# Pooled attention and a gated spatial MLP on one core: the last tokens' scores of two pairs join the second pair's, and the order tables are written anew

## The chip, the cores and the metric

One core of a Trainium2 chip runs the whole program. The metric is the device time of one execution in microseconds, from runs on the chip; the median of three runs of the kernel before is the reference point.

The engines are named as in the profile: PE (matrix multiplications; PEld is its weight loads), DVE (vector), ACT (scalar and activation), POOL (general purpose) and SP, which issues all transfers.

## The reference

```python
# q, k, v: (8 batches, 8 heads, 576 tokens, 64)
k_p = k.reshape(B, H, 72, 8, 64).mean(axis=3)      # keys pooled by 8
v_p = v.reshape(B, H, 72, 8, 64).mean(axis=3)      # values pooled by 8
scores = np.matmul(q, k_p.transpose(0, 1, 3, 2)) / 8
attn = np.exp(scores - scores.max(-1, keepdims=True))
attn = attn / (attn.sum(-1, keepdims=True) + 1e-9)
x = np.matmul(attn, v_p)            # then (8, 576, 512), heads side by side
h = np.maximum(x @ w_in, 0)         # 512 -> 1024
u, v = h[..., :512], h[..., 512:]
v_n = (v - v.mean(-1)) / np.sqrt(v.var(-1) + 1e-6)
v_s = np.einsum('ts,bsd->btd', w_spatial, v_n) + b_spatial[:, None]
out = (u * v_s) @ w_out             # 512 -> 512
```

## The kernel before

**Tiles.** Each of the eight batches goes through attention and then through the MLP. Eight heads make four pairs (g = 0 to 3), two pairs make a j. The 576 tokens are four tiles of 128 and a last piece of 64 (`TL`). There are 72 pooled keys (`SP`). Most products are made of a high and a low part in fp32r, so a value is first rounded (ACT writes the high part, DVE or POOL the low one); scores and transposes are plain fp32.

**Stages.** Each stage is a Python generator, and each `yield` cuts it into steps. `K` and `V` load keys and values and pool them by 8: on PE with `^` behind the name (`pool_pe`: eight matmuls with the identity, L302), on DVE or POOL otherwise (`pool_sum`: three additions, L291 and L296). `KT` transposes the pooled keys into `kT`. `Q0` to `Q3` load a pair's queries and transpose them: `qT` for the four full tiles, `ql` (tile `pt_q`) for the last 64 tokens of the pairs of one j.

`S0` to `S3` (`att_softmax`, L501) make the scores of a pair's four tiles, sixteen matmuls of 64 x 64, into the PSUM tile `s_ps`, and take the softmax. `U0` and `U1` (`att_softmax_l`, L514) do the same for the last 64 tokens of the two pairs of one j: four matmuls into `s_ps` and a softmax of their own. Each `S` and each `U` so has a maximum, exponentials, a sum, a reciprocal (DVE and ACT), one multiplication on POOL (L490), and a copy of the last columns. With a mark behind the name (`S2~`) the exponentials run on ACT straight from `s_ps`, one instruction for each of the eight (or two) rows of a tile; without it DVE first subtracts the maximum and ACT takes one instruction. There is one `s_ps` (two banks), so a group of scores waits until the softmax ahead of it has read the one before.

`T` and `Y` transpose the weights of attention (through DRAM, from batch 2 on), `W` rounds the values, `A00` to `A13` (L647 to L650) multiply them into `xT`. In the MLP, `v0` to `v4` (L699, L715) make the v half and its normalisation (the power on POOL, L686; the low part `vn_l` on POOL, L709), `u` (L742) the u half, `s` (L761 to L763) the spatial product and the gate, `o` (L784) the output. `wv`, `wu`, `wo`, `ws` load the weights; with `^` the low part is made on PE (L223 to L225), without it on POOL.

**Order.** Nothing is scheduled by a tool: `manual_schedule` keeps, on each engine, the order in which the program is written. That order is three tables of stage names: `FIRST` (start, weights and batches 0 and 1), `STEP` (run for each batch 1 to 6) and `LAST` (batch 7). Each name runs the next step of that stage; `+` and `-` shift the batch, and a name whose generator has ended does nothing. So an instruction stands in its engine's queue where the table puts it, and waits there, with all that is behind it, until its operands are ready.

Of the kernel before, what the change touches and what calls it, by code (L numbers as in the profile page):

```python
# [8 lines left out]
F32 = mybir.dt.float32  # L9
# [68 lines left out]
def pooled_attention_gmlp(ctx: ExitStack, tc: tile.TileContext, q, k, v, w_in, w_sp, b_sp, w_out, out):  # L78
    nc = tc.nc
    B, H, S, D = q.shape  # L80
    P = 128
# [216 lines left out]
    def pool_pe(st, dst):  # L298

        m = dst.shape[0]  # L300
        for j in range(POOL):
            nc.tensor.matmul(dst, lhsT=ident[:m, :m], rhs=st[:, :, j * D:(j + 1) * D], start=j == 0, stop=j == POOL - 1)  # L302
# [562 lines left out]
```

## Time and profile before

| what | us |
|---|---|
| median of three runs (556.33 to 556.9) | 556.41 |
| the profiled execution's own time | 556.75 |
| its span in the trace | 554.9 |
| PE busy in the span | 539.7 |
| DVE busy | 374.7 |
| ACT busy | 291.6 |
| POOL busy | 229.4 |

The time of an execution lies 1.85 us above the span of its trace. An engine's busy time is the union of its instructions: matmuls overlap one another, so a stretch in which PE is always busy can still be shortened, by fewer columns or fewer breaks between groups. The distance from one start to the next shows this, not the duration of one instruction.

### The profile page before, as it was taken

The page shows a single profiled execution, that of the slowest core. Times are in us where ns is not written, and L with a number is a line of the kernel's source. Part 1 is how long each engine was busy: PE and PEld are TensorE (multiplying, and loading weights), DVE is VectorE, ACT ScalarE, POOL GpSimd, SP SyncE. Part 2 cuts the span into 40 slices and gives each one's busy share as a digit, 9 for nine tenths or more (in the row PEclk, how much of TensorE's full clock was granted, in tenths as well). Part 3 has the DMA queues.
Part 4 walks back from the last instruction along what each step waited for, and adds up shares of the span by engine and source line. Part 5 has one row for each costly group of instructions (what it writes and reads, how often), then busy time and mean ns, then how long its engine had stood idle before and what let it go on. Part 6 is the DMA issues. An engine that isn't in the chain of part 4 may idle for free.

```text
span 554.9 us, 11870 instructions
## 1 busy us (share of the span) xinstructions
PE 539.7 (97%) x4297; PEld 479.1 (86%) x4297; DVE 374.7 (68%) x930; ACT 291.6 (53%) x916; POOL 229.4 (41%) x316
## 2 busy tenths in 40 slices
PE   4899999999999999999999999999999999999997
PEld 4687788988998889988998889988998889989995
DVE  4589999879766286869687586869687675544010
ACT  3598679743635545373645546364645565425221
POOL 3636754864654234342424224342525126117130
PEclk9999999999999999999999999999999999999999
DMA  8958525537604317342555327342634420201102
GB/s 239 277 180 178 134 90 118 140 102 240 150 11 109 129 45 197 94 126 79 133 140 155 121 57 209 89 127 68 147 87 124 141 57 26 58 0 39 40 1 96
DMA packets 123355, 63.11 MB, mean 114 GB/s; under 512 B 84256, under 2 KB 104736, under 8 KB 123296
## 3 DMA queue, kind: packets, MB, share of 16 engines
q1 hardware_dynamic: 123296, 62.35, 41.8%
q8 instruction: 34, 0.56, 0.4%
q14 instruction: 25, 0.20, 0.1%
HBM read 44.92 MB, written 17.40 MB: 112 GB/s over the span
## 4 chain that ended last, share of the span: by engine, by line
PE 89%; DVE 5%; ACT 2%; DMA 1%; issue 1%; POOL 1%; SPq 1%; DVEq 0%; ACTq 0%
PE mm L761 19%; PE mm L784 18%; PE mm L742 17%; PE mm L699 16%; PE s_ps L501 4%; PE mm L715 2%; PE tp L647 2%; PE mm L762 2%; PE mm L763 2%; PE tp L650 1%; PE tp L649 1%; PE tp L648 1%; DMA st<-in_k 1%; PE mm L302 1%; PE s_ps L514 1%
## 5 line engine op out<-in xcount | busy, mean ns | idle before, releaser
L742 PE MATMUL mm<-xT,win_h 128*128 128x320 f32 (+1 forms) x512 | 104.1, 298 | 0.4 <-DVE wT_l L167 0.4
L775 POOL TENSOR_TENSOR gT<-g,gT 128x256 fp32r<-128x256 f32 x64 | 47.1, 745 | 125.4 <-ACT gT L772 125.3
L742 PEld LDWEIGHTS mm<-xT,win_h 128*128 128x128 f32 x512 | 81.9, 188 | 3.0 <-DVE wT_l L167 0.6
L699 PE MATMUL mm<-win_h,xT 128*128 128x512 f32 x256 | 80.4, 395 | 0.0
L784 PE MATMUL mm<-wout_h,gT 128*128 128x512 f32 x256 | 80.4, 395 | 0.0
L761 PE MATMUL mm<-wT_h,vn_h 128*128 128x256 f32 (+1 forms) x256 | 76.5, 299 | 0.0
L761 PE MATMUL mm<-wT_l,vn_h 128*128 128x256 f32 (+1 forms) x256 | 75.5, 295 | 0.0
L761 PE MATMUL mm<-wT_h,vn_l 128*128 128x256 f32 (+1 forms) x256 | 75.4, 294 | 0.0
L742 PE MATMUL mm<-xT,win_l 128*128 128x256 f32 (+1 forms) x256 | 75.1, 293 | 0.0
L490 POOL TENSOR_TENSOR e<-e,rs 128x576 f32<-128x576 f32 (+1 forms) x48 | 44.3, 924 | 72.2 <-DVE rs L488 36.5
L483 ACT ACTIVATE e<-s_ps,mx 128x72 f32<-128x72 f32 x164 | 50.1, 332 | 20.3 <-DVE mx L469 18.7
L699 PEld LDWEIGHTS mm<-win_h,xT 128*128 128x128 f32 x256 | 47.1, 188 | 10.2 <-ACT win_l L227 0.2
L784 PEld LDWEIGHTS mm<-wout_h,gT 128*128 128x128 f32 x256 | 46.9, 188 | 9.9
L686 POOL TENSOR_TENSOR rstd<-rstd,neg_half 128x1 f32<-128x1 f32 (+1 forms) x40 | 24.8, 622 | 70.1 <-DVE rstd L684 70.1
L766 DVE TENSOR_TENSOR g<-mm,ru 128x256 f32<-128x256 f32 (+1 forms) x64 | 28.0, 447 | 36.1 <-PE mm L763 33.6
L167 DVE TENSOR_TENSOR xT<-tp,xT 128x320 fp32r<-128x320 f32 (+1 forms) x64 | 28.5, 447 | 33.2 <-ACT xT L165 32.8
L709 POOL TENSOR_TENSOR vn_l<-vv,vn_h 128x512 fp32r<-128x512 f32 x32 | 41.6, 1316 | 21.9 <-ACT vn_h L707 21.8
L784 PE MATMUL mm<-wout_l,gT 128*128 128x512 f32 x128 | 50.4, 394 | 0.0
L699 PE MATMUL mm<-win_l,xT 128*128 128x512 f32 x128 | 50.3, 393 | 0.0
L761 PEld LDWEIGHTS mm<-wT_h,vn_h 128*128 128x128 f32 x256 | 48.1, 188 | 1.0 <-DVE wT_l L285 0.3
L761 PEld LDWEIGHTS mm<-wT_h,vn_l 128*128 128x128 f32 x256 | 48.2, 188 | 0.1
L761 PEld LDWEIGHTS mm<-wT_l,vn_h 128*128 128x128 f32 x256 | 48.1, 188 | 0.0
(186 smaller groups left out, 1231.2 us busy)
## 6 DMA issues: line engine op xcount, KB each, us to landing
st<-in_k SPq DMA_DIRECT2D x32, 256.0 KB, 4.1
out<-ob SPq DMA_DIRECT2D x32, 256.0 KB, 2.0
qt<-in_q SPq DMA_DIRECT2D x112, 72.0 KB, 2.5
st<-in_v SPq DMA_DIRECT2D x24, 256.0 KB, 3.3
xd<-X SPq DMA_DIRECT2D x24, 256.0 KB, 2.9
pt_l<-xd SPq DMA_DIRECT2D x24, 256.0 KB, 3.4
stw<-in_moe_w_in SPq DMA_DIRECT2D x8, 512.0 KB, 5.7
st<-in_moe_w_out SPq DMA_DIRECT2D x4, 512.0 KB, 7.3
```

Source lines behind the costliest of these rows:

```text
L167: nc.vector.tensor_tensor(lo, src, f32(hi), op=ALU.subtract)
L483: nc.scalar.activation(em[:, h, :], sv[:, h % 2, h // 2, :], AF.Exp, bias=mx[:, h:h + 1], scale=QK, accum_out=sm[:, h:h + 1])
L490: nc.gpsimd.tensor_tensor(em, em, rs.unsqueeze(2).broadcast_to([m, n, SP]), op=ALU.mult)
L501: nc.tensor.matmul(s_ps[i * TL:(i + 1) * TL, e, c * SP:(c + 1) * SP], lhsT=t["q", g][es, at:at + TL], rhs=kT[es, g, :], start=True, stop=True)
L686: nc.gpsimd.tensor_tensor(rstd[:m], rstd[:m], neg_half[:m], op=ALU.pow)
L699: nc.tensor.matmul(a, lhsT=xT[:, i, o + c * P:o + (c + 1) * P], rhs=w[:, i, DH:], start=(i == 0 and j == 0), stop=(i == NK - 1 and j == 2))
L709: nc.gpsimd.tensor_tensor(t["vn_l"][:, c, :], vv, f32(t["vn_h"][:, c, :]), op=ALU.subtract)
L742: nc.tensor.matmul(a, lhsT=w[:, i, d * P:(d + 1) * P], rhs=xT[:, i, o + ts.start:o + ts.stop], start=(i == 0 and j == 0), stop=(i == NK - ...
L761: nc.tensor.matmul(a, lhsT=x[:, c, ds], rhs=y[:, c, ts], start=(c == 0 and j == 0), stop=False)
L766: nc.vector.tensor_tensor(g, a, t["ru"][:, d, ts], op=ALU.mult)
L775: nc.gpsimd.tensor_tensor(dst[:, d, 1, at:at + m], g[:, o:o + m], f32(dst[:, d, 0, at:at + m]), op=ALU.subtract)
L784: nc.tensor.matmul(a, lhsT=src[:, i, x, at:at + m], rhs=w[:, i, :], start=(i == 0 and j == 0), stop=(i == ND - 1 and j == 2))
```

## The change

The stages `U0` and `U1` are gone. `S1` and `S3`, the scores of the second pair of each j, have a fifth tile: the last 64 tokens of both pairs of that j, from `ql`. It lies in the same `s_ps`, and one softmax takes all ten rows of a tile; the tiles `mx`, `e`, `sm` and `rs` grow from eight to ten. `S0` and `S2` stay as they were.

```diff
     def att_softmax(t, g, alt=""):
...
-        for c in range(NC):
+        j, odd = divmod(g, 2)
+        n = NC + odd
+
+        for c in range(n):
             for i in range(2):
                 for e in range(2):
                     es, at = slice(e * D, (e + 1) * D), c * P + i * TL
-                    nc.tensor.matmul(s_ps[i * TL:(i + 1) * TL, e, c * SP:(c + 1) * SP],
-                                     lhsT=t["q", g][es, at:at + TL], rhs=kT[es, g, :], start=True, stop=True)
-        yield
-        em = yield from softmax(s_ps[:, :, :4 * SP].rearrange("p e (c s) -> p e c s", s=SP), P, 8, alt)
-        nc.gpsimd.tensor_copy(new_pr(t, g // 2)[:, :NC, :, g % 2], em[:, 1::2, SP - KR:])
-        t["p", g] = em
-
-    def att_softmax_l(t, j, alt=""):
-
-        sl = ps.tile([P, 2, 512], F32, name="s_ps", tag="s")
...
+                    lhs, pair = (t["q", g][es, at:at + TL], g) if c < NC else (t["ql", j][es, i, :], 2 * j + i)
+                    nc.tensor.matmul(s_ps[i * TL:(i + 1) * TL, e, c * SP:(c + 1) * SP], lhsT=lhs, rhs=kT[es, pair, :],
+                                     start=True, stop=True)
+        yield
+        em = yield from softmax(s_ps[:, :, :n * SP].rearrange("p e (c s) -> p e c s", s=SP), 2 * n, alt)
+        pr = new_pr(t, j)
+        nc.gpsimd.tensor_copy(pr[:, :NC, :, odd], em[:, 1:2 * NC:2, SP - KR:])
+        t["p", g] = em[:, :2 * NC, :]
+        if odd:
+            nc.gpsimd.tensor_copy(pr[:TL, NC, :, 0], em[:TL, 2 * NC + 1, SP - KR:])
+            yield
+            nc.scalar.copy(pr[:TL, NC, :, 1], em[TL:, 2 * NC + 1, SP - KR:])
+            t["pl", j] = em[:, 2 * NC:, :]
```

A new mark `%` for `K` and `V` would halve the pooling on PE by one addition ahead of it; the new tables give it to no `K` and no `V`, so `pool_half` adds nothing here. The three tables are written anew. The first entries of `FIRST`:

```diff
-    "wv0 wv0 wv0 -K^ wv3~^ -K -K wv3 wv0 -K wv3 wv0 -Q1^ wo1^! -K wv3 -K wv0 -Q0~^ wv3 -K -KT -Q0 wo1 wo1 -KT "
+    "wo1~ -K^ -K wo1 wo1 wo1 -K wv1 -Q0~^ -K wv1 wo1 -K -Q0 wv1 -K wo1 -K wv3^! wv3 -Q1^ wv1 wv1 -KT~ -Q0 -KT "
```

By the new tables five weight chunks instead of six are rounded on PE (three matmuls fewer: `x`, a high part and `z`), and pooling moves between engines: of the halves of `K` and `V` that are summed by `pool_sum`, DVE has 6 instead of 22 and POOL 18 instead of 2. What is pooled on PE stays the same in number.

**PE in the middle of the program, before.** `pt_q` holds the last tokens' queries, `qT` the other tokens'; the wide products with `xT` belong to the stages `u` and `v`.

```order
L742 MATMUL mm<-xT,win_h 128x256 x2
L742 MATMUL mm<-xT,win_l 128x256
L514 MATMUL s_ps<-kT,pt_q 64x72 x4
L742 MATMUL mm<-xT,win_h 128x320 x2
L742 MATMUL mm<-xT,win_l 128x320
```

The same place in the change:

```order
L734 MATMUL mm<-win_h,xT 128x512
L734 MATMUL mm<-win_l,xT 128x512
L530 MATMUL s_ps<-kT,qT 64x72 x16
L530 MATMUL s_ps<-kT,pt_q 64x72 x4
L761 MATMUL mm<-xT,win_h 128x320 x2
L761 MATMUL mm<-xT,win_l 128x320
```

The four matmuls of the last tokens now follow the sixteen of the second pair, with no wide product between them; each of the sixteen groups of before does so.

**PE at the start, before** (`st` and `st_r` are raw keys, `kp` and `kr` pooled ones, `qt` raw queries, `x` a weight chunk):

```order
L302 MATMUL mm<-st,ident 128x128 x16
L302 MATMUL mm<-st_r,ident 64x64 x8
L223 MATMUL mm<-x,ident 128x512
L224 MATMUL mm<-win_h,ident_m 128x512
L225 MATMUL mm<-z,ident_p 128x512
L348 MATMUL tp<-ident,kp 128x128 x2
L349 MATMUL tp<-ident,kr 128x64
L444 MATMUL tp<-ident,qt 128x128 x4
L445 MATMUL tp<-ident,qt 128x64
L444 MATMUL tp<-ident,qt 128x128 x4
L445 MATMUL tp<-ident,qt 128x64
L501 MATMUL s_ps<-kT,qT 64x72 x16
```

In the change:

```order
L321 MATMUL mm<-st,ident 128x128 x16
L467 MATMUL tp<-ident,qt 128x128 x4
L468 MATMUL tp<-ident,qt 128x64
L321 MATMUL mm<-st_r,ident 64x64 x8
L369 MATMUL tp<-ident,kp 128x128 x2
L370 MATMUL tp<-ident,kr 128x64
L467 MATMUL tp<-ident,qt 128x128 x4
L468 MATMUL tp<-ident,qt 128x64
L530 MATMUL s_ps<-kT,qT 64x72 x16
L467 MATMUL tp<-ident,qt 128x128 x4
L468 MATMUL tp<-ident,qt 128x64
L530 MATMUL s_ps<-kT,qT 64x72 x16
```

The first weight chunk has left the place between pooling and `KT`, the first queries stand ahead of the keys' rest, and only one transpose of queries stands between the first two groups of scores.

**POOL from a batch's first normalisation to its first spatial product, before** (`rstd` is a power, `vn_l` a low part, `e` the multiplication of a softmax):

```order
L686 TENSOR_TENSOR rstd_2886<-rstd_2886,neg_half_77 128x1
L490 TENSOR_TENSOR e_2888<-e_2888,rs_2921 128x576
L505 COPY pt_p_2937<-e_2888 128x64
L686 TENSOR_TENSOR rstd_2927<-rstd_2927,neg_half_77 128x1
L686 TENSOR_TENSOR rstd_2989<-rstd_2989,neg_half_77 64x1
L709 TENSOR_TENSOR vn_l_2746<-vv_2785,vn_h_2745 128x512
L709 TENSOR_TENSOR vn_l_2746<-vv_2833,vn_h_2745 128x512
L709 TENSOR_TENSOR vn_l_2746<-vv_2860,vn_h_2745 128x512
L709 TENSOR_TENSOR vn_l_2746<-vv_2898,vn_h_2745 128x512
```

The end of that stretch in the change:

```order
L301 TENSOR_TENSOR st_3577<-st_3577 128x2x256
L301 TENSOR_TENSOR st_3577<-st_3577 128x2x128
L306 TENSOR_TENSOR kp_3372<-st_3577 128x128
L513 TENSOR_TENSOR e_3621<-e_3621,rs_3689 128x576
L535 COPY pt_p_3701<-e_3621 128x64
L705 TENSOR_TENSOR rstd_3698<-rstd_3698,neg_half_77 128x1
L728 TENSOR_TENSOR vn_l_3545<-vv_3614,vn_h_3544 128x512
L301 TENSOR_TENSOR st_r_3651<-st_r_3651 64x256
L301 TENSOR_TENSOR st_r_3651<-st_r_3651 64x128
L306 TENSOR_TENSOR kr_3373<-st_r_3651 64x128
L705 TENSOR_TENSOR rstd_3818<-rstd_3818,neg_half_77 64x1
L728 TENSOR_TENSOR vn_l_3545<-vv_3572,vn_h_3544 128x512
```

Between the powers and the low parts now stand the sums of the next batch's keys (`st`, `kp`, `st_r`, `kr`), most of which DVE had before.

## Rows read from the trace of the kernel before

**Rows 1.** the page: its first line and the engines' busy time

```profile
span 554.9 us, 11870 instructions
...
PE 539.7 (97%) x4297; PEld 479.1 (86%) x4297; DVE 374.7 (68%) x930; ACT 291.6 (53%) x916; POOL 229.4 (41%) x316
```

**Rows 2.** stretches: length, then PE, PEld, DVE, ACT, POOL busy (instructions), clock, DMA

```profile
0.00:20.00 20.00, 12.05 (x106) 10.16 (x107) 7.86 (x21) 7.65 (x16) 8.78 (x13) 1.00 0.89 260
20.00:40.00 20.00, 17.19 (x228) 14.37 (x226) 15.54 (x41) 16.26 (x62) 10.52 (x12) 1.00 0.68 205
...
260.00:320.00 60.00, 60.00 (x489) 53.93 (x488) 43.06 (x110) 31.89 (x103) 21.40 (x33) 1.00 0.48 129
```

**Rows 3.** what PE waited for (line waited for: us in total, times, longest)

```profile
PE mm L302 <- DMA st<-in_k: 7.9, 2, 6.6
PE s_ps L514 <- ACT e L483: 1.1, 1, 1.1
PE s_ps L501 <- DVE e L475: 1.0, 1, 1.0
PE s_ps L514 <- DVE e L475: 0.7, 1, 0.7
```

**Rows 4.** timeline of PE around a last-token group of scores (start us, us)

```profile
205.41 0.39 PE L742 MATMUL mm<-xT,win_h 128*128 128x256 f32 x2
205.64 0.28 PE L742 MATMUL mm<-xT,win_l 128*128 128x256 f32 x1
205.85 0.36 PE L514 MATMUL s_ps<-kT,pt_q 64*64 64x72 f32 x8
206.13 0.56 PE L742 MATMUL mm<-xT,win_h 128*128 128x320 f32 x2
```

**Rows 5.** the same around the next main group of scores

```profile
210.71 0.28 PE L742 MATMUL mm<-xT,win_l 128*128 128x256 f32 x1
210.92 0.73 PE L501 MATMUL s_ps<-kT,qT 64*64 64x72 f32 x32
211.58 0.50 PE L742 MATMUL mm<-xT,win_h 128*128 128x256 f32 x2
211.92 0.28 PE L742 MATMUL mm<-xT,win_l 128*128 128x256 f32 x1
```

**Rows 6.** the same around one rounding of a weight chunk on PE

```profile
41.03 1.13 PE L223 MATMUL mm<-x,ident 128*128 128x512 f32 x2
...
42.46 0.28 PE L647 MATMUL tp<-pt_h,vm_h 128*128 128x256 f32 x1
```

**Rows 7.** timeline of PE, ACT and DVE in the start

```profile
11.70 2.02 PE L302 MATMUL mm<-st,ident 128*128 128x128 f32 x16 [1.32 <-DMA st<-in_k]
13.65 1.14 PE L302 MATMUL mm<-st_r,ident 64*64 64x64 f32 x16
...
15.10 0.26 ACT L342 COPY kr<-mm 64x128 f32<-64x128 f32 x1
...
18.31 0.73 PE L501 MATMUL s_ps<-kT,qT 64*64 64x72 f32 x32
...
20.00 0.75 DVE L467 TENSOR_REDUCE mx<-s_ps 128x8 f32<-128x576 f32 x1
20.78 0.76 DVE L475 TENSOR_TENSOR e<-s_ps,mx 128x576 f32<-128x576 f32 x1
```

**Rows 8.** fetches of the queries in the first 40 us, from issue to landing

```profile
DMA to landing us min/median/max: 3.4/5.0/7.6
```

**Rows 9.** timeline of POOL: two sums of values, and three low parts; then PE

```profile
133.59 2.10 POOL L291 TENSOR_TENSOR st<-st 128x512 f32<-128x512 f32 x2 [3.20 <-DVE xT L167]
...
149.81 3.75 POOL L291 TENSOR_TENSOR st<-st 128x512 f32<-128x512 f32 x2
...
213.90 3.81 POOL L709 TENSOR_TENSOR vn_l<-vv,vn_h 128x512 fp32r<-128x512 f32 x3 [2.72 <-ACT vn_h L707]
...
218.95 0.31 PE L761 MATMUL mm<-wT_h,vn_h 128*128 128x320 f32 x1
```

More of the change, by code (lines that the diff above doesn't have):

```diff
@@ L296, in pool_sum, with pool_half, pool_pe @@
         eng.tensor_tensor(dst, x, y, op=ALU.add)
[L298 to L302, printed above, removed]
+    def pool_half(sts, alt):
+        if "%" in alt:
+            for st in sts:
+                x = st[:, :, :POOL * D // 2]
+                eng = nc.vector if "^" in alt else nc.gpsimd
+                eng.tensor_tensor(x, x, st[:, :, POOL * D // 2:], op=ALU.add)
+                yield
+    def pool_pe(st, dst, alt):
+        m, n = dst.shape[0], POOL // 2 if "%" in alt else POOL
+        for j in range(n):
+            nc.tensor.matmul(dst, lhsT=ident[:m, :m], rhs=st[:, :, j * D:(j + 1) * D], start=j == 0, stop=j == n - 1)
     def ps_pool():
@@ L328, in att_keys @@
         yield
+        pe = "^" in alt or "%" in alt
+        yield from pool_half((*sts, st), alt)
         for r in range(2):
-            if "^" in alt:
+            if pe:
                 acc = acc if r else ps_pool()
-                pool_pe(sts[r], acc[:, 2 * r:2 * r + 2, :])
+                pool_pe(sts[r], acc[:, 2 * r:2 * r + 2, :], alt)
             else:
@@ L335, in att_keys @@
             yield
-        if "^" not in alt:
+        if not pe:
             pool_sum(st, kr, nc.gpsimd if alt else nc.vector)
         else:
-            pool_pe(st, acc[:2 * RR, NG:, :])
+            pool_pe(st, acc[:2 * RR, NG:, :], alt)
             yield
@@ L378, in att_values @@
         yield
+        pe = "^" in alt or "%" in alt
+        yield from pool_half((*sts, st), alt)
         for r in range(2):
-            if "^" in alt:
+            if pe:
                 acc = acc if r else ps_pool()
-                pool_pe(sts[r], acc[:, g2[r], :])
+                pool_pe(sts[r], acc[:, g2[r], :], alt)
             else:
@@ L385, in att_values @@
             yield
-        if "^" not in alt:
+        if not pe:
             pool_sum(st, vq, eng)
         else:
-            pool_pe(st, acc[:2 * RR, NG:, :])
+            pool_pe(st, acc[:2 * RR, NG:, :], alt)
             yield
@@ L461, in new_pr, with softmax @@
         return t["r", j]
-    def softmax(sv, m, n, alt):
-        mx = ring("mx", 2, [P, 8], F32, "mx")[:m, :n]
+    def softmax(sv, n, alt):
+        mx = ring("mx", 2, [P, 10], F32, "mx")[:, :n]
         mv = mx.rearrange("p (c e) -> p e c", e=2)
@@ L470, in softmax @@
         yield
-        em = ring("e", 3, [P, 8, SP], F32, "e")[:m, :n, :]
+        em = ring("e", 3, [P, 10, SP], F32, "e")[:, :n, :]
         ev = em.rearrange("p (c e) s -> p e c s", e=2)
-        sm = ring("sm", 2, [P, 8], F32, "sm")[:m, :n]
+        sm = ring("sm", 2, [P, 10], F32, "sm")[:, :n]
         if not alt:
@@ L500, in att_softmax @@
                     es, at = slice(e * D, (e + 1) * D), c * P + i * TL
-                    nc.tensor.matmul(s_ps[i * TL:(i + 1) * TL, e, c * SP:(c + 1) * SP],
-                                     lhsT=t["q", g][es, at:at + TL], rhs=kT[es, g, :], start=True, stop=True)
+                    lhs, pair = (t["q", g][es, at:at + TL], g) if c < NC else (t["ql", j][es, i, :], 2 * j + i)
+                    nc.tensor.matmul(s_ps[i * TL:(i + 1) * TL, e, c * SP:(c + 1) * SP], lhsT=lhs, rhs=kT[es, pair, :],
+                                     start=True, stop=True)
         yield
-        em = yield from softmax(s_ps[:, :, :4 * SP].rearrange("p e (c s) -> p e c s", s=SP), P, 8, alt)
-        nc.gpsimd.tensor_copy(new_pr(t, g // 2)[:, :NC, :, g % 2], em[:, 1::2, SP - KR:])
-        t["p", g] = em
-    def att_softmax_l(t, j, alt=""):
-        sl = ps.tile([P, 2, 512], F32, name="s_ps", tag="s")
-        for i in range(2):
-            for e in range(2):
-                es = slice(e * D, (e + 1) * D)
-                nc.tensor.matmul(sl[i * TL:(i + 1) * TL, e, :SP], lhsT=t["ql", j][es, i, :],
-                                 rhs=kT[es, 2 * j + i, :], start=True, stop=True)
-        yield
-        em = yield from softmax(sl[:, :, :SP].unsqueeze(2), P, 2, alt)
-        nc.gpsimd.tensor_copy(new_pr(t, j)[:TL, NC, :, 0], em[:TL, 1, SP - KR:])
-        yield
-        nc.scalar.copy(new_pr(t, j)[:TL, NC, :, 1], em[TL:, 1, SP - KR:])
-        t["pl", j] = em
+        em = yield from softmax(s_ps[:, :, :n * SP].rearrange("p e (c s) -> p e c s", s=SP), 2 * n, alt)
[7 more added lines that the diff above has]
+            t["pl", j] = em[:, 2 * NC:, :]
     def new_pt(t, j):
@@ L669, in attention @@
         for j in range(NG // 2):
-            st[f"U{j}"] = lambda j=j, **alt: att_softmax_l(t, j, **alt)
             st[f"T{j}"] = lambda j=j, **alt: att_pt(t, b, j, **alt)
```

4 lines of the change are left out of this document (2 added, 2 removed), and 86 rows, old and new, of tables (FIRST, LAST, STEP).

## The prediction

> **What bounds the kernel now.** I read the engines' busy time on the page first, then the busy time by stretches, then what PE waited for, and last PE's own timeline around the instructions that the change touches.
>
> PE is busy 539.7 of 554.9 us, every other engine 68% or less [rows 1]. The 15.2 us that are missing are not spread out: 8.0 lie in the first 20 us, 2.8 in the next 20, and a stretch from the middle shows 60.00 of 60.00 [rows 2]. Most of the other 4.4 is the copy and store behind the last matmul, which the change leaves alike. What PE waits for at the start is listed: keys, 7.9 us in two waits of which the longest, 6.6, is the first fetch of all; and three waits of 1.1, 1.0 and 0.7 us ahead of groups of scores, for a softmax that still reads the only `s_ps` [rows 3]. From then on the kernel is one row of PE work, and only two things can shorten it: fewer columns, or fewer breaks between groups. The clock is no part of it: the granted clock is 1.00 in all three stretches, the 2.4 GHz level [rows 2].
>
> That PE reads as always busy doesn't mean that it streams all the time, because matmuls overlap in the trace. So I take the distances between starts. Wide products of 256 columns start 0.115 us apart (two in 0.23, from 205.41 to 205.64) [rows 4].
>
> **The last tokens' groups.** Around a lone group of last-token scores the wide products' starts stand 205.64 and 206.13, so 0.49 us where 0.115 would do [rows 4]. Around a main group they stand 210.71 and 211.58, 0.87 us; and behind it the next two take 0.34 (211.58 to 211.92) where two take 0.23 elsewhere, 0.11 more [rows 5]. I take this 0.11 for the small group too. So a lone last-token group costs 0.49 - 0.115 + 0.11 = 0.485 us of PE, and a main group 0.865. The first has 8 records and the second 32 [rows 4, 5]: 0.38 us for 24 records, 0.016 each. The other 0.36 us is paid once for going from wide products to small ones and back. As a fifth tile the eight records cost 8 x 0.016 = 0.13. **Each merged group saves 0.485 - 0.13 = 0.36 us.**
>
> There are sixteen such groups. Two stand in the start among PE's waits and are counted there. Of the other fourteen, twelve stand between wide products, by the order of before, and two have another small group on one side; for these I take half. 12 x 0.36 + 2 x 0.18 = 4.7 us. All of it lies on the path, since PE does nothing else there. Bounds: if the eight records take as long inside as alone (205.85 to 206.13, 0.28 us [rows 4]), 0.2 is left of each of the twelve, 2.5 us in all; if they cost nothing, 12 x 0.485 + 2 x 0.28 = 6.4.
>
> Whether the break is really paid once depends on what the array counts as one group: the fifth tile has other weights and another pair's keys. No row shows a fifth tile. The Trainium skill (TensorEngine Tiling (Array Packing), Key Properties) says that changing the tiling mode drains TensorE, and changing the tile alone does not. By that rule the sum stands as above; by a break at each change of operands it would be that of rival 3. The trace agrees as far as it goes: the 0.36 us appears between 128-row and 64-row products [rows 4, 5].
>
> **The softmax of these groups.** DVE, ACT and POOL lose sixteen small maxima, sums, reciprocals and multiplications, and sixteen of the remaining ones grow from eight rows to ten. None of that is on the path in the middle, where PE never waits [rows 2]. I cost it at nothing; its cover is PE's own work. The bound is the wait for `s_ps` in rows 3, about 1 us at a group. In the new order at least forty wide products, over 4.6 us at 0.115, stand between two groups of scores in the middle, while a softmax holds `s_ps` for some 2.7 us at the start (below). Before, fourteen stood there at the closest.
>
> **One weight chunk less on PE.** Rounding a chunk there takes from 41.03 to 42.46, 1.43 us [rows 6]. Its two steps go to POOL, which has time ahead of the first use. Saving 1.4, between 0 (if PE then waits anyway) and 1.4.
>
> **The start.** Here PE waits, so what counts is which wait ends last. I walked the new order in rows of before. The first fetch is again one weight chunk and then the first keys: 6.6 us as before [rows 3]. The second half of the keys is now issued ahead of the second weight chunk, so the 1.32 us wait [rows 7] goes. The waits of 0.7, 1.0 and 1.1 us [rows 3] go as well, two with their groups and one because pooling and a weight chunk (over 3 us) now stand ahead of it. Removed: 1.32 + 0.7 + 1.0 + 1.1 = 4.1.
>
> New waits: `KT` stands directly behind the pooling of the keys' rest, with two ACT copies between (pooling ended at 14.79, the second copy at 15.36 [rows 7]): 0.5. The first scores wait for the rest of `kT`, which DVE writes behind a step on the third weight chunk: 0.3. The second group of scores has one transpose group (0.9 us) between it and the first, where `s_ps` is free only after DVE's maximum and subtraction, 0.75 and 0.76 us [rows 7] and the hops between, some 1.8; and this transpose needs the third queries, whose fetch is issued only when the first queries are transposed, at 13 to 15, and lands a median 5.0 later [rows 8]. I take 2.0 for both. The rounding of the weight chunk behind it waits 0.3 for POOL. Sum 3.1 to 3.2. **The start gains 0.9 us.** Bounds: no new wait at all, 4.1 gained; or fetches of the queries at the slowest 7.6 [rows 8], 2.6 later, at two of the four pairs in part: 3 lost.
>
> **Pooling moves from DVE to POOL.** Off the path as long as POOL keeps up; the one place to watch is the low part of the last `v` ahead of the first `s`. Before, three low parts ended at 213.90 + 3.81 = 217.71, and the first `s` began at 218.95 [rows 9]: 1.2 us to spare, and POOL had been idle for 2.72 just ahead. The new order puts the sums of the keys, some 6 us, among these; it also moves the v groups forward, with seven groups of PE work, about 10 us by widths, between the last `v` and the first `s`. POOL is busy 21.4 of 60 us in the middle [rows 2]. I take nothing; the loss is rival 2.
>
> **Sum.** The profiled execution took 556.75 us, 1.85 above its span. 556.75 - 4.7 - 1.4 - 0.9 = **549.8 us**. The median of the runs, 556.41, lies 0.34 below the profiled execution; I leave the forecast where the sum puts it.
>
> **Rivals.**
>
> 1. The start loses: the second group of scores waits for late queries behind it in PE's queue. For it: PE's order leaves only one transpose between the first two groups, and the fetch behind it can't start early. Against it: most of the waits of rows 3 are gone with their groups. Start +3 instead of -0.9: 553.7.
>
> 2. POOL becomes the bound ahead of the first `s`. The same pair of additions took 2.10 us once and 3.75 another time [rows 9], 1.8 times as long. The Trainium skill (SBUF — State Buffer, SBUF: two separate sides) says that DVE and GpSimd share one pair of ports under an exclusive lock, held for the whole instruction. That speaks against moving additions to POOL; the two durations in rows 9 agree with it, and it would make this rival's time. If the keys' sums, 6 us, all stretch so, the chain grows by 4.7; with 1.2 to spare PE waits 3.5 in each of the four batches whose keys are on POOL by the new order: 14 us, 563.8, slower than before. It decides from about 2 us of wait a batch. Against it: POOL was idle two thirds of a batch, and DVE now has less to do.
>
> 3. The merge doesn't shorten PE: the fixed 0.36 is paid again at the fifth tile. Then 1.4 + 0.9 remain: 554.4.
>
> **How the numbers follow.** Chances: the forecast 0.66 (547 to 552.5, the bounds of the merge and the start in part), rival 1 0.16, rival 3 0.08, rival 2 0.08, below 547 0.02. The range 547 to 554.5 holds the forecast, rival 1 and rival 3, and leaves out rival 2, the ends of the bounds, and half of what stands near 554. A measurement here can tell 0.2%, 1.1 us, from no change. Faster by more than that: 0.66 + 0.02 + nearly all of rivals 1 and 3, 0.20: 0.88. Within it 0.04, from rivals that come out together. Slower 0.08, rival 2.
>
> **What would show it.** In the profile after: wide products 0.99 us apart around a group of twenty score matmuls (0.87 + 0.13); no wait of PE for `s_ps` in the middle; PE busy near 533; waits of PE at the start of about 10 us in all, the first fetch included, the longest of the others at the second group of scores. A wait of the first `s` for POOL means rival 2; a distance of 1.3 us around the merged group means rival 3. I am wrong if PE waits after the first 60 us for more than 1 us in all, or if the merged group costs more than 1.1 us.

## The result, and the profile after

| | before | after |
|---|---|---|
| median of four runs each, us | 556.37 | 551.54 |
| lowest and highest run | 556.19, 556.9 | 551.36, 552.11 |
| profiled execution, us | 556.75 | 551.63 |
| span of its trace | 554.9 | 549.8 |

The ratio of after to before is 0.9913, 95% interval 0.9896 to 0.993. The kernel is 4.8 us faster. The forecast was 549.8, with a range of 547.0 to 554.5 and a chance of 0.88 for faster: the direction and the range held, and the time came out 1.7 above the forecast. The profiled execution gained 5.1 us where the sum had 7.0.

The busy times on the page of after answer [rows 1]. PE is busy 4.8 us less. The forecast wanted it near 533. DVE lost 34.7 us and POOL gained 49.0.

```profile
PE 534.9 (97%) x4293; PEld 477.8 (87%) x4293; DVE 340.0 (62%) x785; ACT 291.6 (53%) x958; POOL 278.4 (51%) x375
```

The stretches of after (length, then PE, PEld, DVE, ACT, POOL busy, clock, DMA) answer [rows 2]. In the middle PE is busy 60.00 of 60.00 again, at a granted clock of 1.00 as before. In the first 20 us it is busy less than before (11.45 against 12.05), in the next 20 more (18.37 against 17.19).

```profile
0.00:20.00 20.00, 11.45 (x131) 9.98 (x135) 8.60 (x24) 7.20 (x13) 9.22 (x15) 1.00 0.76 223
20.00:40.00 20.00, 18.37 (x223) 15.22 (x215) 13.81 (x32) 15.49 (x59) 12.64 (x13) 1.00 0.81 266
260.00:320.00 60.00, 60.00 (x491) 54.16 (x482) 35.70 (x81) 29.96 (x102) 32.85 (x47) 1.00 0.45 123
```

What PE waited for in after (line waited for: us in total, times, longest) answers [rows 3]. Each of these waits stands in the first 50 us; behind that this view lists none. The three waits ahead of groups of scores, 2.8 us, have become one of 1.0 for `s_ps` and one of 0.2 for `kT`, and the second wait for the keys is gone. Beside the first fetch there are eight short waits now, 4.5 us in all.

```profile
PE mm L321 <- DMA st<-in_k: 6.5, 1, 6.5
PE s_ps L530 <- DVE e L498: 1.0, 1, 1.0
PE tp L667 <- DVE xT L177: 0.7, 1, 0.7
PE mm L233 <- POOL x L213: 0.7, 1, 0.7
PE tp L467 <- DMA qt<-in_q: 0.5, 1, 0.5
PE mm L235 <- POOL z L224: 0.5, 1, 0.5
PE tp L369 <- ACT kp L362: 0.5, 1, 0.5
PE tp L628 <- ACT pt_p L540: 0.4, 1, 0.4
PE s_ps L530 <- DVE kT L379: 0.2, 1, 0.2
```

The weight loads (PEld) have a list of their own. It names two waits ahead of spatial products that the list of PE leaves out. The rows behind it are PE at the first spatial product (L780) of one batch:

```profile
PEld mm L780 <- ACT ru L764: 0.9, 4, 0.2
...
PEld mm L780 <- POOL vn_l L728: 0.5, 2, 0.3
```

```profile
275.11 0.31 PE L761 MATMUL mm<-xT,win_l 128*128 128x320 f32 x1
275.38 0.42 PE L780 MATMUL mm<-wT_h,vn_h 128*128 128x320 f32 x1
275.63 0.31 PE L780 MATMUL mm<-wT_h,vn_l 128*128 128x320 f32 x1
```

The starts stand 0.27 and 0.25 us apart where 0.15 is usual, so 0.22 us are lost. It is the same in four batches (at 214.97, 275.38, 338.61 and 399.01), 0.9 in all. In batch 0 a spatial product waits for POOL's low part, and the distances there (85.33, 85.74, 85.97) are together 0.4 longer than usual. In before the first spatial product followed without a gap (218.81, 218.95, 219.10).

PE around a merged group in the middle (start us, us) answers [rows 4, 5]. The wide products on both sides stand 1.11 us apart (199.01 to 200.12). A product of 512 columns alone takes 0.23 (198.78 to 199.01), and the next two, of 320, take 0.40 where two take 0.29 elsewhere (one 0.15, 200.52 to 200.67), 0.11 more. So the merged group costs 1.11 - 0.23 + 0.11 = 0.99 us, as forecast. The twelve merged groups that stand between wide products all lie at 0.98 to 0.99 by this reckoning.

```profile
198.78 0.39 PE L734 MATMUL mm<-win_h,xT 128*128 128x512 f32 x1
199.01 0.40 PE L734 MATMUL mm<-win_l,xT 128*128 128x512 f32 x1
199.34 0.73 PE L530 MATMUL s_ps<-kT,qT 64*64 64x72 f32 x32
199.89 0.31 PE L530 MATMUL s_ps<-kT,pt_q 64*64 64x72 f32 x8
200.12 0.56 PE L761 MATMUL mm<-xT,win_h 128*128 128x320 f32 x2
200.52 0.31 PE L761 MATMUL mm<-xT,win_l 128*128 128x320 f32 x1
200.67 0.46 PE L761 MATMUL mm<-xT,win_h 128*128 128x320 f32 x2
```

To see in which part the time was gained, I take the first product of the first gating stage and the last matmul of each kernel, in PE's timeline: first the two rows of before, then the last output stage ahead of that product in after, and the two rows of after.

```profile
55.59 0.72 PE L699 MATMUL mm<-win_h,xT 128*128 128x512 f32 x2
...
550.83 0.40 PE L784 MATMUL mm<-wout_l,gT 128*128 128x512 f32 x1
```

```profile
54.39 0.31 PE L667 MATMUL tp<-pt_h,vm_h 128*128 128x320 f32 x1
...
54.99 0.62 PE L718 MATMUL mm<-win_h,xT 128*128 128x512 f32 x2
...
545.68 0.40 PE L803 MATMUL mm<-wout_l,gT 128*128 128x512 f32 x1
```

The first gating product starts 0.60 us earlier. In the new order one more output stage stands ahead of it (54.39 to 54.99, 0.60), so the start gained 1.2. From that product to the last matmul it was 495.24 us and is now 490.69, 4.55 less. Of this 0.60 is the stage that went ahead, so the merge and the rest of the new order gained 3.95 there. What follows the last matmul took as long as before (4.07 and 4.12).

The start was to gain 2.3 (0.9 by waits, 1.4 by the chunk) and gained 1.2. The part behind it was to gain 4.7 and gained 3.95.

### The profile page after: what moved, and what is told of

It is laid out like the page before. It is cut to its first block, busy times and chain, and to the rows that moved or that the text cites. A ratio compares the mean times of both kernels' runs of the same rounds, so it can differ in the third digit from the quotient of the medians.

```text
span 549.8 us, 11810 instructions
## 1 busy us (share of the span) xinstructions
PE 534.9 (97%) x4293; PEld 477.8 (87%) x4293; DVE 340.0 (62%) x785; ACT 291.6 (53%) x958; POOL 278.4 (51%) x375
## 4 chain that ended last, share of the span: by engine, by line
PE 89%; POOL 3%; ACT 2%; DMA 2%; issue 1%; DVE 1%; SPq 1%; POOLq 0%; ACTq 0%; DVEq 0%
PE mm L780 19%; PE mm L803 18%; PE mm L761 17%; PE mm L718 16%; PE s_ps L530 4%; PE mm L734 2%; DMA qt<-in_q 2%; PE tp L667 2%; PE tp L670 2%; PE mm L781 2%; PE mm L782 2%; PE tp L669 1%; PE tp L668 1%; PE mm L321 1%; POOL vn_l L728 1%
## 5 line engine op out<-in xcount | busy, mean ns | idle before, releaser
L780 PE MATMUL mm<-wT_h,vn_h 128*128 128x256 f32 (+1 forms) x256 | 77.3, 302 | 0.0
L780 PE MATMUL mm<-wT_h,vn_l 128*128 128x256 f32 (+1 forms) x256 | 75.9, 297 | 0.1
L780 PE MATMUL mm<-wT_l,vn_h 128*128 128x256 f32 (+1 forms) x256 | 75.6, 295 | 0.0
L761 PE MATMUL mm<-xT,win_l 128*128 128x320 f32 (+1 forms) x256 | 75.2, 294 | 0.0
L705 POOL TENSOR_TENSOR rstd<-rstd,neg_half 128x1 f32<-128x1 f32 (+1 forms) x40 | 23.2, 583 | 68.3 <-DVE rstd L703 68.2
L506 ACT ACTIVATE e<-s_ps,mx 128x72 f32<-128x72 f32 x190 | 57.6, 332 | 0.2
L728 POOL TENSOR_TENSOR vn_l<-vv,vn_h 128x512 fp32r<-128x512 f32 x32 | 43.0, 1354 | 28.0 <-ACT vn_h L726 28.0
L791 ACT ACTIVATE gT<-g 128x256 fp32r<-128x256 f32 x64 | 25.8, 413 | 47.0 <-DVE g L785 47.0
L699 DVE BATCH_NORM_STATS2 st<-vv 128x6 f32<-128x512 f32 (+1 forms) x40 | 27.3, 682 | 37.7 <-ACT vv L722 37.6
L780 PEld LDWEIGHTS mm<-wT_h,vn_h 128*128 128x128 f32 x256 | 48.2, 188 | 2.0 <-ACT ru L764 0.9
L780 PEld LDWEIGHTS mm<-wT_h,vn_l 128*128 128x128 f32 x256 | 48.3, 189 | 0.8 <-POOL vn_l L728 0.5
```

The source lines that it names most:

```text
L506: nc.scalar.activation(em[:, h, :], sv[:, h % 2, h // 2, :], AF.Exp, bias=mx[:, h:h + 1], scale=QK, accum_out=sm[:, h:h + 1])
L699: nc.vector.bn_stats(st6[:m], vv[:m])
L705: nc.gpsimd.tensor_tensor(rstd[:m], rstd[:m], neg_half[:m], op=ALU.pow)
L728: nc.gpsimd.tensor_tensor(t["vn_l"][:, c, :], vv, f32(t["vn_h"][:, c, :]), op=ALU.subtract)
L761: nc.tensor.matmul(a, lhsT=w[:, i, d * P:(d + 1) * P], rhs=xT[:, i, o + ts.start:o + ts.stop], start=(i == 0 and j == 0), stop=(i == NK - ...
L780: nc.tensor.matmul(a, lhsT=x[:, c, ds], rhs=y[:, c, ts], start=(c == 0 and j == 0), stop=False)
```

## Experiments

Twelve kernels were run, each timed in five rounds against the kernel before on the same chip. The medians of before differed from session to session (556.9 to 557.5), so ratios are compared, and differences in us are taken from them with before at 556.4. One more thing has to be taken out of single traces: the wait for the first keys. In the kernels that have the transfers in the order of after it was 6.3 us in one trace and 8.1 in another.

### The merge: e1_split, e2_merge_only, e7_merge_from2

**e1_split.** The fifth tile is set apart again by one wide stage.

```diff
         for c in range(n):
+            if c == NC and t["b"] > 1:
+                yield
...
             next(parts.get(key, iter(())), None)
+            if new and key[1] in ("S1", "S3") and key[0] > 1:
+                late.append(key)
+            elif new and late and key[1][0] in "vusoA":
+                for again in (late.pop(), *kept):
+                    next(parts[again], None)
+                kept.clear()
```

> The kernel after, with the fifth tile's 4 matmuls of both odd pairs' scores in batches 2 to 7 set apart from the four main tiles by one other wide TensorE stage (12 groups of twenty become 12 of sixteen and 12 of four); softmax, its steps and all tables stay, the maximum of these pairs comes behind the fifth tile. Theory (TensorE pays 0.36 us for each trip wide - small - wide, whatever the softmax does): 12 x 0.36 = 4.3 us more, 555.8 us, ratio to the kernel before 0.999; the lone group of four records again at a distance of 0.48 to 0.50 from its wide neighbours' grid and the main group at 0.85 to 0.87. Rival (the gain of the merge came from fewer softmax instructions on DVE and ACT, or from the new orders): 551.5 to 552.0, ratio 0.991.

Measured: 556.32 us, ratio 0.9989 (0.9978 to 1.0001). Against after that is 4.2 us more, most of the 4.8 that the change gained. PE's timeline around one of the groups set apart:

```profile
202.70 0.30 PE L763 MATMUL mm<-xT,win_l 128*128 128x320 f32 x1
202.93 0.36 PE L532 MATMUL s_ps<-kT,pt_q 64*64 64x72 f32 x8
203.22 0.72 PE L720 MATMUL mm<-win_h,xT 128*128 128x512 f32 x2
203.78 0.40 PE L720 MATMUL mm<-win_l,xT 128*128 128x512 f32 x1
```

From 202.70 to 203.22 it is 0.52 us where 0.15 is usual between products of 320 columns, and the next two products of 512 columns take 0.56 where 0.46 is usual: 0.47 for eight records, as the lone group of before in [rows 4]. The softmax is the merged one here, and DVE and ACT do what they do in after. Twelve such groups make 12 x (0.47 - 0.13) = 4.1 us. In the first 25 us the waits differ from those of after, with a granted clock of 0.50 from 20 to 23 us, but the same group of scores starts at 25.34 us in both traces. Behind that PE waits some 0.5 us more at the output stages (two waits for `xT`) and 0.5 at the spatial products (three of at most 0.2 for ACT), so up to 1 us of the 4.2 may be theirs. The price belongs to PE's trip from wide products to small ones and back, and neither to the softmax nor to the order tables.

**e2_merge_only.** The tables of before, with the merged scores and softmax. The tokens of `U` do nothing, and before the first step of a `Y` the steps of its `S` that are left are run.

```diff
-            st[f"U{j}"] = lambda j=j, **alt: att_softmax_l(t, j, **alt)
...
+            if key[1] in ("Y0", "Y1") and (key[0], f"S{2 * int(key[1][1]) + 1}") in parts:
+                for _ in parts[key[0], f"S{2 * int(key[1][1]) + 1}"]:
+                    pass
```

> The kernel before, with its own tables, in which the scores' fifth tile and the one softmax are put in as in the kernel after (the steps of the lone last-token scores do nothing now); the sixth weight chunk stays on TensorE and all pooling stays where it was. Theory: the merge by itself brings its own term, 12 x 0.36 us in batches 2 to 7 and 0.2 to 0.4 at the start, 4.5 to 4.7 us: 551.7 to 551.9, ratio 0.992, unless the longer softmax, for which these tables left no room, is waited for (then less, and the wait stands in TensorE's waits at s_ps). Rival (the orders made anew brought the gain, the merge alone brings little): 555 to 556.4, ratio 0.998 to 1.

Measured: 558.13 us, ratio 1.0011 (0.9995 to 1.0028): no gain. The number is the rival's. PE's waits show where much of it went:

```profile
PE tp L603 <- POOL e L490: 2.9, 1, 2.9
PE s_ps L507 <- DVE e L475: 1.4, 1, 1.4
PE tp L549 <- POOL e L490: 0.8, 1, 0.8
```

In the tables of before the lone softmax stood early, and its transposes (L603) soon behind it. Now they need the last step of the pair's merged softmax on POOL, and wait 2.9 us for it. I had looked for the wait at `s_ps`; it stands one stage further on. These waits lie in batches 0 and 1, whose softmax and transposes on PE follow each other closely.

The waits are not all of it. Behind the one of 2.9 us the granted clock lay near 0.50, the 1.2 GHz level, for some 3 us (length, busy times as above, then clock and DMA):

```profile
29.40:32.60 3.20, 3.20 (x16) 3.19 (x16) 0.90 (x4) 2.86 (x16) 2.97 (x2) 0.53 0.26 102
```

The sixteen pooling matmuls there take 3.31 us from their first start to the next product (29.41 to 32.72), where the same sixteen take 1.89 in before (27.05 to 28.94). All twelve executions of e2 have a mean clock of 0.991 to 0.996, those of before 0.996 to 1.0. So a part of what e2 lost, 1.4 us and more in this trace, is the lower clock.

**e7_merge_from2.** The same, but merged only from batch 2 on.

```diff
+            merge = b > 1 and g % 2
-            st[f"S{g}"] = lambda g=g, **alt: att_softmax(t, g, **alt)
+            st[f"S{g}"] = lambda g=g, f=att_softmax_m if merge else att_softmax, **alt: f(t, g, **alt)
...
+            if b < 2:
                 st[f"U{j}"] = lambda j=j, **alt: att_softmax_l(t, j, **alt)
```

> The kernel before with its own tables, merged as in e2_merge_only but only from batch 2 on; batches 0 and 1, whose transposes waited 2.9 and 0.8 us for the merged pair's last step in e2, keep the lone last-token scores. Theory (each merged group saves 0.36 us of TensorE, and what e2 lost stands at the start): 12 x 0.36 = 4.3 us less than before, 552.1 to 552.5, ratio 0.992. Rival (the merge in these orders loses as much by waits in every batch): 555.5 to 557, ratio 0.998 to 1.002.

Measured: 553.03 us, ratio 0.9929 (0.9912 to 0.9945), 4.0 us less than before, where 4.3 was expected. So the twelve merged groups bring their 0.36 each in the old tables too, and what e2 lost, it lost in the first two batches. The new order of the start is what makes the merge possible there. It isn't the source of the merge's gain.

### The weight chunk: e3_chunk_back

```diff
-    ... -T1 -T1 -T1 wu3~ -T1 KT ...
+    ... -T1 -T1 -T1 wu3~^ -T1 KT ...
```

> The kernel after, with the weight chunk wu3 of the start rounded on TensorE again (the sixth such chunk; POOL's two steps for its low part go, ACT gets one copy). Theory: 1.4 us more, the distance of such a group in the trace (41.03 to 42.46 in the trace of before), 552.9 to 553.0, ratio 0.994, since TensorE is without a gap around its place. Rival (POOL is late near the start, so that POOL's share of it was on the path as well): 551.0 to 551.6, ratio 0.990.

Measured: 552.88 us, ratio 0.9929 (0.9908 to 0.9951), 0.9 us above after, with a span 0.8 longer (550.6). In its trace the chunk that was put back takes 1.44 us of PE (62.74 to 64.18), as forecast. The sign and size of the measured time speak for the theory too, but the two intervals overlap, so that all of the 1.4 reaches the end is neither shown nor excluded.

### The pooling on POOL: e8_k_dve, e11_before_k_pool

**e8_k_dve** puts the keys' sums in the steady steps back on DVE.

```diff
-    ... -Y1 +K! V -A00 ...
+    ... -Y1 +K V -A00 ...
```

> The kernel after, with the pooling of the keys in the steady steps (the steps of table STEP, 3 sums in each of 5 batches) back on VectorE from POOL. Theory (neither engine bounds TensorE there, VectorE is busy 340 of 550 us and POOL 278): within 0.5 us of after, 551.1 to 552, ratio 0.991. Rival 1 (the move to POOL was needed so that VectorE releases the scores in time): 1 to 3 us more, ratio 0.993 to 0.997. Rival 2 (POOL was on the edge, as the prediction's second rival has it): 0.5 to 2 us less, ratio 0.988 to 0.990.

Measured: 555.96 us, ratio 0.998 (0.9968 to 0.9991), 3.7 us above after. (The sums of three batches change, not of five: DVE has 27 instructions more, nine a batch.) The theory fell. PE's waits of e8, then PE at one of the places, then ACT and DVE there:

```profile
PE mm L780 <- ACT ru L764: 4.3, 3, 1.4
```

```profile
277.45 0.42 PE L780 MATMUL mm<-wT_h,vn_h 128*128 128x320 f32 x1 [1.44 <-ACT ru L764]
```

```profile
275.98 0.63 ACT L748 ACTIVATE vt<-vv 64x512 fp32r<-64x512 f32 x1 [1.34 <-DVE vv L707]
...
277.04 0.36 ACT L764 ACTIVATE ru<-mm 128x256 f32<-128x256 f32 x1
```

```profile
267.13 0.71 DVE L301 TENSOR_TENSOR st_r<-st_r 64x256 f32<-64x256 f32 x2
...
274.35 1.60 DVE L707 TENSOR_SCALAR vv<-vv,mv,rstd 64x512 f32<-64x512 f32 x1
```

PE waits three times for 1.4 us, at the first spatial product, for ACT's copy of a `u` group (L764). That copy stands in ACT's queue behind the rounding of the last `v` (L748), which waits for DVE's normalisation (L707 at 274.35). In after this instruction starts at 272.26, 2.1 us earlier. Of this 0.6 is the later place of the whole trace (PE's last `u` product starts at 275.70 here and at 275.11 there); the other 1.5 is DVE's delay, with the keys' sums (L301) ahead of the normalisation in its queue. In after the same copy is late already by the 0.22 us shown above, so there is no room that could take the delay up. The place is the one that the prediction named for rival 2, the last `v` ahead of the first `s`. But the move to POOL relieves it, and doesn't load it.

**e11_before_k_pool** is the counterpart: before, with the same sums on POOL.

```diff
-    ... -u12 -S3 +K -Y0 ...
+    ... -u12 -S3 +K! -Y0 ...
```

> The kernel before with its own tables, with the key pooling sums of three batches in the steady steps on POOL in place of VectorE (the counterpart of e8_k_dve, which put them back in the kernel after and lost 3.7 us). Theory (the move is worth something only in the new orders, in which VectorE's statistics of the normalisation stand behind these sums and the first gating stage right behind them): nothing, within 0.5 us of before, ratio 0.999 to 1.001. Rival 1 (the move is a gain by itself, and part of what was put down to the merge): 1 to 3 us less, ratio 0.994 to 0.998. Rival 2 (POOL becomes late for the scores in these orders): over 1 us more, ratio above 1.002.

Measured: 556.84 us, ratio 0.9989 (0.9977 to 1.0001). Nothing that can be told from no change. So the move is worth nothing in the old order and 3.7 us in the new one.

### The start: e4_sign_dve, e5_sign_v, e6_s1_later, e9_wu0_late, e10_all, e12_exp_first

Three of the longer waits of after were not in the prediction, or smaller there: 0.7 and 0.5 us at the rounding of a weight chunk, and 0.7 at an output stage (L667). PE's rows of the chunk in after (in brackets the idle time ahead and what ended it), then POOL and DVE for it:

```profile
23.03 1.13 PE L233 MATMUL mm<-x,ident 128*128 128x512 f32 x2 [0.74 <-POOL x L213]
...
24.87 0.49 PE L235 MATMUL mm<-z,ident_p 128*128 128x512 f32 x1 [0.48 <-POOL z L224]
```

```profile
19.57 2.04 POOL L212 TENSOR_SCALAR stw<-stw 128x512 int32<-128x512 int32 x1
21.69 1.28 POOL L213 TENSOR_TENSOR x<-x,stw 128x512 int32<-128x512 int32 x1
23.51 1.30 POOL L224 TENSOR_TENSOR z<-stw,y 128x512 fp32r<-128x512 f32 x1 [0.54 <-DVE y L218]
```

```profile
23.01 0.43 DVE L218 TENSOR_SCALAR y<-x 128x512 uint32<-128x512 uint32 x1 [1.75 <-POOL x L213]
```

The chunk `wv3` takes its sign on POOL, 2.04 and 1.28 us. DVE waits 1.75 us for this ahead of its next step (23.01), POOL's product `z` comes behind that, and PE waits for both.

**e4_sign_dve** makes this sign step on DVE.

```diff
+            if "~" in alt:
                 sign, xw = high.bitcast(I32), x.bitcast(I32)
                 nc.gpsimd.tensor_scalar(sign, sign, 0.0, -2.0 ** 31, op0=ALU.is_lt, op1=ALU.mult)
                 nc.gpsimd.tensor_tensor(xw, xw, sign, op=ALU.add)
+            else:
+                nc.vector.scalar_tensor_tensor(xi, high, 0x80000000, xi, op0=ALU.bitwise_and, op1=ALU.bitwise_or)
```

> The kernel after, with the sign step of the one early weight chunk wv3 on VectorE (one instruction) in place of POOL (two instructions, 2.04 and 1.28 us at 19.6 to 23.0 us in the trace of after). Theory (the start loses what it was to gain to POOL's path in this chunk): the waits of TensorE for POOL's x and z, 0.7 and 0.5 us and the 1 us of rounding between them that runs stretched, go in part: 0.7 to 1.7 us less, 549.8 to 550.8, ratio 0.988 to 0.990. Rival (what is late next, the loads of the keys or the scores' release by VectorE, takes the time back, or VectorE's step holds the scores up): 551.2 to 552, ratio 0.991 to 0.992.

Measured: 550.45 us, ratio 0.9882 (0.9862 to 0.9902), 1.7 us below after by the ratios (1.1 by the bare medians); the two intervals overlap by a little. In the trace both waits for POOL are gone, and the wait for `pt_p` too; those for `s_ps` (1.0) and at the output stage (0.7) are as in after. DVE's instruction that takes the place of the two on POOL:

```profile
19.00 0.94 DVE L216 SCALAR_TENSOR_TENSOR x<-stw,x 128x512 uint32<-128x512 uint32 x1
```

The first gating product starts at 53.16 us, 1.8 earlier than in after, though the wait for the first fetch was no shorter (7.0 here, 6.5 and 0.5 for the queries there).

**e5_sign_v** is e4 with a pooling step of the values put ahead of the fourth output stage (`K -A00 V` becomes `K V -A00`), which waits 0.7 us for the split of the first.

> The kernel of e4_sign_dve, with one TensorE step of the values' pooling (16 records, 1.8 us) put ahead of the fourth of the first four output stages, which in e4 waits 0.75 us at 39.8 us for VectorE's split of the first of them (three transposing buffers, the fourth stage needs the first back). Theory: that wait is filled with work that comes next anyway: 0.7 us less than e4, about 549.7, ratio 0.987. Rival (VectorE and ACT are late as a whole there, by the ten exponentials of the merged softmax, so that the wait comes back at the next transposes): as e4, 550.4, ratio 0.988.

Measured: 550.63 us, ratio 0.9885 (0.9868 to 0.9902), as e4. The wait only moved, to the next user of the three transposing buffers:

```profile
PE tp L579 <- DVE xT L177: 0.8, 1, 0.8
```

**e6_s1_later** is e5 with a pooling step put ahead of the second group of scores (`K^ -S1 -V -V` becomes `K^ -V -V -S1`).

> The kernel of e5_sign_v, with the first pooling step of the values on TensorE put ahead of the second group of scores, which waits 0.96 us at 19.2 us for VectorE's subtraction of the first group. Theory A (a wait is only filled as far as the next one allows): the weight chunk's group behind it comes 1 us earlier and then waits for its part from POOL, which is there at 22.7 us: 0.2 to 0.4 us less than e5. Theory B: the values have not landed at 18.3 us, the step waits for its DMA instead, up to 1 us; no gain, or a loss of up to 1 us. Theory C: the whole 0.96 us is gained.

Measured: 550.13 us, ratio 0.9875 (0.9858 to 0.9891): 0.5 us below e5 at best, within the intervals. The wait for `s_ps` halves, to 0.5, and one for the values' transfer takes the place of the other half. The number lies near theory A, the mechanism is that of B, with a smaller loss:

```profile
PE mm L324 <- DMA st<-in_v: 0.7, 1, 0.7
```

**e9_wu0_late** takes the steps of a weight chunk out of ACT's and DVE's queues ahead of the output stages. **e10_all** does the same on top of e6.

```diff
-    ... -W wu0 K -T0 ... -S3 -A01 wu0 V ... -S3 ws1 -T1 ... wv0 wu0 wu1 -A03 ... -A03 wv0 ... v0 v2 S1
+    ... -W K -T0 ... -S3 -A01 V ... -S3 ws1 wu0 -T1 ... wv0 wu1 -A03 ... -A03 wu0 wv0 ... v0 wu0 v2 S1
```

> The kernel of e4_sign_dve, with the steps of the weight chunk wu0 on ACT (1.35 us) and VectorE (1.55 us), which in e4 stand ahead of the ten exponentials of the last scores and of VectorE's split of the first output stage, moved some 10 us later (its part is used only by the gating stages behind 60 us). Theory (in the stretch 30 to 40 us of the start ACT and VectorE are the late ones, and the wait of 0.75 us at 39.8 us is their backlog, which no other order of TensorE's steps takes away, as e5 showed): the wait goes, 0.5 to 0.8 us less than e4, about 549.8, ratio 0.987. Rival (the backlog comes back at the next transposes, as in e5): as e4, 550.4, ratio 0.988.

> The kernel of e6_s1_later with the same steps of wu0 moved as in e9_wu0_late, so all the edits to the start that were tried: sign step of wv3 on VectorE, a pooling step ahead of the fourth output stage and one ahead of the second group of scores, wu0 later. Theory: the gains add, e6 (0.9875) less 0.7 us: ratio 0.986, 549.4. Rival: no more than e6 or e4, ratio 0.9875 to 0.988.

Measured: 554.41 us, ratio 0.9944 (0.9923 to 0.9964), and 553.95 us, ratio 0.9943 (0.9924 to 0.9962). Both theories fell: some 3.5 us lost. In e9 the wait at the output stage is 0.6 instead of 0.7, and new ones stand behind the first gating products, where ACT and DVE now have the chunk's steps as well:

```profile
PE mm L764 <- ACT ru L767: 1.7, 1, 1.7
PE mm L236 <- ACT vv L725: 1.6, 1, 1.6
```

**e12_exp_first.** In after, ACT's split of the first output stage comes straight behind the ten exponentials of the last scores:

```profile
40.34 0.37 ACT L506 ACTIVATE e<-s_ps,mx 128x72 f32<-128x72 f32 x1
...
40.64 1.09 ACT L175 ACTIVATE xT<-tp 128x256 fp32r<-128x256 f32 x3
```

This kernel is e4 with the exponentials moved ahead of a rounding step for which they had been held back, and `wu0` moved by 10 us alone.

```diff
-    ... -W wu0 K -T0 ... -Y0 -Y0 -S3 -A01 wu0 V -A01 ... -S3 ws1 -T1 -T1 -T1 KT
+    ... -W K -T0 ... -S3 -Y0 -Y0 -A01 V -A01 ... -S3 ws1 wu0 -T1 wu0 -T1 -T1 KT
```

> The kernel of e4_sign_dve, with the ten exponentials of the last scores of batch 0 on ACT put ahead of the last rounding step of the short transposes, and the steps of the weight chunk wu0 on ACT and VectorE moved only 10 us later, behind the first four output stages, with all its later steps in their old places (in e9 these were moved too and cost over 3 us behind 60 us). Theory (the wait of 0.75 us at 39.8 us for the first output stage's split is the ten exponentials, 3 us, that stand just ahead of this split in ACT's queue and wait there for the short transposes' step): the exponentials run from 34 to 37 us, the split at 37.8, the wait goes and the first gating product starts 0.5 to 0.8 us earlier than in e4 against the landing of the first keys; ratio 0.987 (e4: 0.9882). Rival (any order of these steps has its backlog elsewhere): the wait comes back at the next transposes or at a product of the gating stages, ratio 0.988 or above.

Measured: 554.35 us, ratio 0.9943 (0.9923 to 0.9962). The wait at the fourth output stage is gone, which speaks for the exponentials' place in ACT's queue as its cause (with `wu0` alone moved, in e9, 0.6 of it stayed). But a longer one comes ten us later:

```profile
PE tp L673 <- DVE pt_rr L590: 2.9, 1, 2.9
```

DVE's `pt_rr` of the next pair stands behind the moved steps. And behind this wait PE worked at a granted clock of 0.50, the 1.2 GHz level, for nearly 6 us (columns as above):

```profile
52.20:58.00 5.80, 5.80 (x45) 3.79 (x45) 3.83 (x12) 2.50 (x10) 0.61 (x1) 0.50 0.44 77
```

From the product that waited to the first gating product it takes 7.68 us (52.16 to 59.84), and in e4 5.16 for the same work (48.00 to 53.16), so 2.5 more. All six executions have a mean clock of 0.987 to 0.997, where e4's have 0.999 or 1.0. So the loss against e4 is the new wait and the lower clock, and not the wait alone. In e4 the longest gap between 30 and 60 us is 1.3 us on ACT and 1.0 on DVE, and each of four attempts moved the backlog to another wait or added one. That 0.7 us can be had at all was not shown.

## Why the prediction was right, and where it was off

**What bounds the kernel: right in the main.** The list of PE's waits has none behind 50 us in after. But the distances between starts show 1.3 us lost ahead of spatial products, 0.9 for ACT and 0.4 for POOL's low part. The prediction called itself wrong for more than 1 us of waits behind 60 us: by PE's list that has not come, by the distances it has, just.

**The merged group: right in mechanism and size.** 0.99 was forecast and measured. e1 adds a break at each group and pays 4.2 us, of which 1 may be new waits; e7 takes the lone groups away in the old order and gets 4.0. Rival 3 is excluded: the fifth tile has other weights and other keys, and pays no second break. The Trainium skill (TensorEngine Tiling (Array Packing), Key Properties) says that a change of tiling mode drains TensorE and a change of tile alone does not; the trace agrees, with 0.13 us for the fifth tile within the group and 0.47 for the same eight records set apart.

The part behind the start gained 3.95 where 4.7 was forecast. The 1.3 us just named more than make up the 0.75 that are missing. Against them stands a wait of before for the spatial weights (`wT_l`), which is gone:

```profile
PE mm L742 <- DVE wT_l L167: 0.4, 1, 0.4
```

By the distances it cost 0.6 us (82.86, 83.53, 83.93). My estimate from these rows is 4.7 - 1.3 + 0.6 = 4.0. The two groups with a small neighbour, counted at 0.18 each, were not separated.

**The weight chunk: right on PE, open in the total.** 1.44 us in e3's trace, and 0.9 by the times for 1.4, within the intervals.

**The softmax at nothing: right for this order, with a condition that I didn't see.** In the middle PE never waits for `s_ps`. But in the old order the merge was eaten up by batches 0 and 1 (e2), by waits and by the lower clock behind them. The condition isn't the distance between groups of scores, which I counted, but the one from the second pair's softmax to the transposes that read it.

**The start: wrong, and here the forecast lost 1.1 us.** The step that failed is the sum of new waits, 3.1 to 3.2 forecast and 4.5 measured, so that the start's waits lost 0.4 and didn't gain 0.9. Two of its terms held: keys' transposes 0.5 (forecast 0.5) and first scores 0.2 (0.3). The second group of scores waited 1.0 and not 2.0: it was to wait for a softmax and late queries, and the queries were there in time. The rounding behind it was put at 0.3 for POOL and waited 0.7 and 0.5, since POOL's two sign instructions, 3.3 us, stand ahead of its product. e4, which takes them away, is 1.7 us faster. Not in the sum at all were the fourth output stage (0.7), the first queries (0.5) and the short transposes (0.4). So 2.5 us of waits were missed and 1.1 counted too much; that the total came within 1.7 us is in part luck, because the two errors cancel in part. I walked the new order at PE's waits for the softmax, and three others stood in queues that I didn't walk: ACT's ten exponentials ahead of a split (e12), POOL's sign step, SP's fetch.

Rival 1 said that the start loses at the second group of scores. That group has the longest wait behind the first fetch, but only 1.0, and for DVE.

**The pooling at nothing: the number nearly held, the reason didn't.** PE waits for a low part of POOL only in batch 0, 0.4 us by the distances. In the middle the margin shrank: the last low part ends at 275.03 and the first `s` starts at 275.38, 0.35 later, where [rows 9] had 1.2. The keys' sums on POOL are not stretched: two pairs of additions took 2.17 and 2.11 us, near the 2.10 and not the 3.75 of [rows 9]. I argued that the move costs nothing because POOL has time. e8 and e11 show that it carries 3.7 us of the new order and none in the old one. The place of rival 2, the first `s`, is where the 0.22 us are lost in each of four batches. What is late there is ACT, behind DVE's last normalisation, and that takes 1.61 us in after (272.26) where it took 0.53 in before (212.39). POOL's low part starts 0.04 us behind it (272.30). So POOL may have its share by way of DVE; no run separates this. I had looked at what the move asks of POOL, and not at what DVE would have owed without it.

**The total.** 7.0 forecast and 5.1 gained in the profiled executions: 1.1 is missing at the start and 0.75 behind it.

A version that is at least as fast as both: e4, ratio 0.9882, and e6, 0.9875, against 0.9913 for after. Both are faster than before beyond doubt. e6's interval ends at 0.9891, below that of after (from 0.9896); e4's overlaps it by a little. These kernels and after were timed in different sessions.

## What to carry to other kernels

Where PE is the bound and never waits, look for small groups between wide ones: what is paid is the trip, 0.36 us here, and hardly the records, 0.016 each, so put small products into one group. A list of waits can leave out small ones that come back in every batch; the distances between starts show them. Before merging a softmax, count the distance from its end to whoever reads it. An operation that is moved to another engine is costed from both sides: what it asks of the new engine, and what would stand late on the old one in the new order.

## What the runs showed of the hardware

I had not expected that two POOL instructions for a sign (2.04 and 1.28 us for 128 x 512) would hold what one of DVE does in 0.94 us in e4 (the row above). Nor that PE's granted clock would lie at 0.50, the 1.2 GHz level, behind a wait of 2.9 us in e2 and in e12, for some 3 and 6 us of work, with 1.4 and 2.5 us lost. In e9 waits of 1.7 and 1.6 us had no such stretch behind them; in e1 such a stretch stands behind a wait of 1.0 us, which after has without it. What decides it is not shown here. Nor that a normalisation of DVE (128 x 512) that takes 0.50 us in before (207.80) would take 1.60 where a low part of POOL starts in the same moment (209.86 and 209.88); that POOL is the cause is not tested. Nor that the first fetch of the keys, with the same transfers ahead of it, takes from 6.3 to 8.1 us from trace to trace. A difference of 1 us between two spans means nothing before this is taken out.
